# Placing W1's tables at the right end of SBUF and giving W3's and x's first loads earlier

## The chip, the cores and the metric

The kernel runs on one core of one Trainium2 chip. The metric is device time in microseconds (us) of one execution; lower is better. TensorE does matrix products, VectorE and ScalarE elementwise work, GpSimd a few small steps; SP (SyncE) and ScalarE give the DMA transfers.

## The reference

Three stages on 3072 tokens (4 sequences of 768), all weights in float64 for the host and taken apart on the chip:

```python
# 1. attention in chunks of 32 queries over 8 memory keys and 56 neighbours; 8 heads of 64
a = softmax(q_c @ k_full.T / 8);  x = a @ v_full          # x: 3072 x 512
# 2. first feed-forward: W1 512 x 1024, W2 1024 x 512
h = x @ W1;  solu = h * softmax(h)
x2 = (layernorm(solu) * g_ln) @ W2                        # x2: 3072 x 512
# 3. second feed-forward: W3 512 x 2048, W4 2048 x 512
h3 = x2 @ W3;  g = max(0.01 * h3, h3);  out = g @ W4
```

## The kernel before, in words

Every product is made of float32 parts: an operand is split into a high part (rounded, on ScalarE) and a low part (the rest, on VectorE), and three matmuls, high-high, high-low and low-high, go into one PSUM bank. A table is therefore always a pair such as `w1h`, `w1l`.

**Stages 1 and 2** run over 24 tiles of 128 tokens (`for i in range(NTILE + 1)`). For tile i the loop does attention of tile i+2, `s_h` (product with W1, softmax, LayerNorm: max, exp, product `so`, Square pass `e`/`ve`, `rstd`, scaling of `so`), `s_lt` (transposes, high and low part into `lhl`), a piece of W3's decoding (`load_raw`, `decode_steps`, `store_w3`: W3 is decoded, combined and stored to DRAM as `w3f`), and `s_o` for work i-5: one quarter (`ec`) of the product of a block of 512 tokens with W2 into bank `x2p`. `s_o` copies the bank to `x2s` on ScalarE (L355) and stores it to DRAM, `x2d` (L356). `x2s` has one buffer (`bufs=1`), so a copy waits for the store before it. Four such works (block 5) are left behind the loop: **W2's tail**, 96 matmuls.

**Stage 3** multiplies x2 with W3 and the result with W4 by Strassen-Winograd products P1 to P7. Tokens go in three pairs of blocks (v = 0, 1, 2). `load_xt` loads a pair from `x2d` in four transfers (b12, b22, b11, b21) into `xt` (pair 0) or `xtq` (pair 1), `x_steps` makes the seven operands by four additions or subtractions and seven splits (`split`, L503 on ScalarE, L504 on VectorE). `load_w3` loads a slot (`L0`, `L1`: W3's seven operands of 256 columns), `w3_steps` splits it (L561, L562). A unit is one slot with one pair: unit 0 is L0 with pair 0, unit 1 is L0 with pair 1. TensorE's order within a unit is P1, P5, P4 of the unit before, P6, P3 of the unit before, P2, P7. P1, P6, P7 and P4 add up in one bank C, and ScalarE keeps its state between them (`keep`, L677: s after P1, u after P6, g after P7). So P6 waits for s, P7 for u, P4 for g.

**Order.** Up to W2's tail a list scheduler places the instructions of TensorE, VectorE, ScalarE and GpSimd by the order of the program text and by when it takes operands to be ready; from `order_ctx` on SP's order is that of the text, and from the units on that of all engines. Each engine works through its own list in order. Each transfer adds to one of eight completion counters, given in turn in the order of the text; it waits until the transfer before it on that counter has landed.

**Memory.** A core's memory is a stack from the left and one from the right. Before, `w1h`, `w1l`, `w2h`, `w2l` lie at the left (16 KB per partition each), and L0 to L3 take their place after W2's tail: L0, L1 that of W1, L2, L3 that of W2. `xq` (with `xtq`) takes that of `lhl`. Pair 1's operands for P1, P5, P6, P2 are kept in L2 and L3 until those hold W4. `xr` (operands of pair 0) and `xt` take the place of stage 1's buffers at the right, among them those of W3's staging.

The lines that matter: L355 and L356, L497 (x loads), L503 to L522 (x steps), L553 (W3 load), L561 and L562, L648 (TensorE in stage 3), L677.

Of the kernel before, what the change touches and what calls it, by code (L numbers as in the profile page):

```python
# [9 lines left out]
F32 = mybir.dt.float32  # L10
F32R = mybir.dt.float32r
# [12 lines left out]
LAG = 5  # L24
# [15 lines left out]
def tile_kernel(  # L40
# [13 lines left out]
    P = 128  # L54
    NTILE = qt.shape[0]
# [5 lines left out]
    KD = DM // P  # L61
    KF = DFF // P
    KF2 = DFF2 // P
    BT = 512
    NBLK = NT // BT
    TB = BT // P
# [76 lines left out]


    sa, sh, satt, sps, sx2 = (ExitStack() for _ in range(5))
    wA = sa.enter_context(tc.tile_pool(name="wA", bufs=1, reuse_waits="tile"))
    w1h = wA.tile([P, 2, KD, 512], F32R, name="w1h")
    w1l = wA.tile([P, 2, KD, 512], F32R, name="w1l")
    w2h = wA.tile([P, KF, DM], F32R, name="w2h")
    w2l = wA.tile([P, KF, DM], F32R, name="w2l")  # L150
    sst = ExitStack()
# [45 lines left out]
    def s_scores(i, q, k):  # L197
        sc = ps_att.tile([P, 8, 64], F32, name="att")
        for hp in range(4):
            for c in range(4):  # L200
                cs = slice(32 * c, 32 * c + 32)
                nc.tensor.matmul(  # L202
                    sc[cs, 2 * hp : 2 * hp + 2, :], q[:, hp, cs], k[:, :, hp, c, :],
                    start=True, stop=True,
                )
        if i % TPB == 0:
            nc.vector.memset(sc[0:32, :, 8:24], NEG)
        if i % TPB == TPB - 1:
            nc.vector.memset(sc[96:128, :, 56:64], NEG)
        nms = sm.tile([P, 8], F32, name="nms")  # L210
        nc.vector.tensor_reduce(out=nms, in_=sc, op=ALU.max, axis=AX.X, negate=True)
        nc.vector.tensor_scalar_mul(nms, nms, SCALE)  # L212
        return sc, nms

    def s_exp(sc, nms):
        p = p1.tile([P, 8, 64], F32, name="p")
        rs = sm.tile([P, 8], F32, name="rs")
        for h in range(8):
            nc.scalar.activation(  # L219
                p[:, h], sc[:, h], AF.Exp, bias=nms[:, h : h + 1], scale=SCALE,  # L220
                accum_out=rs[:, h : h + 1],
            )
        return p, rs
# [118 lines left out]
    def s_o(b, ec, lh, ll, part):  # L342
        if part == 0:
            open_x2[ec] = ps_x2.tile([P, BT], F32, name="x2p")
        ps = open_x2[ec]
        es = slice(ec * P, (ec + 1) * P)
        for kk in range(4 * part, 4 * part + 4):
            for n, (a, r) in enumerate(((w2h, lh), (w2h, ll), (w2l, lh))):
                nc.tensor.matmul(  # L349
                    ps, a[:, kk, es], r[:, kk],  # L350
                    start=(kk == 0 and n == 0), stop=(kk == KF - 1 and n == 2),
                )
        if part == 1:
# [27 lines left out]
    for d in LOADS:  # L381
# [3 lines left out]
        n = int(d[1])  # L385
# [24 lines left out]
    lb = {}  # L410
# [20 lines left out]
    for i in range(NTILE + 1):  # L431
        a = i + 2
        b, t = divmod(i, TB)
# [4 lines left out]
        if att:  # L438
            p, rs = s_exp(*s_scores(a, ld[0], ld[1]))
# [13 lines left out]
        if so is not None:  # L453
            j = i - 1
# [10 lines left out]
        if 0 <= i - W3_FROM < KF2:  # L465
            f = i - W3_FROM
# [11 lines left out]
    store_w3(KF2 - 1, w3s)  # L478
    sps.close()
    satt.close()  # L480

    NPAIR, NV = KF2 // 2, NBLK // 2
    tt, pt_ = nc.vector.tensor_tensor, nc.gpsimd.tensor_tensor
    PROD = ("P1", "P5", "P6", "P2", "P7", "P3", "P4")
    SLOT = {"P1": 0, "P2": 1, "P7": 2, "P4": 3, "P5": 4, "P6": 5, "P3": 6}
    ACC = {"P1": "A", "P2": "A", "P5": "B", "P3": "B", "P6": "C", "P7": "C", "P4": "C"}
    ACC3 = {**ACC, "P1": "C"}
    spx, sxr, sxt, sl, sq, sd, sg, s4 = (ExitStack() for _ in range(8))
    ps = spx.enter_context(tc.tile_pool(name="ps_abc", bufs=2, space=PSUM, reuse_waits="tile"))
    xrp = sxr.enter_context(tc.tile_pool(name="xrp", bufs=1, side="right", reuse_waits="tile"))  # L490
    xr = {r: xrp.tile([P, 2, 2, BT], F32R, name=f"x{r}") for r in PROD}
    xtp = sxt.enter_context(tc.tile_pool(name="xtp", bufs=1, side="right", reuse_waits="tile"))

    def load_xt(v, tb):
        t = dict(zip(("b11", "b12", "b22", "b21", "t2"), (tb[:, n : n + 2] for n in range(0, 10, 2))))
        for n, b, k in (("b12", 1, 0), ("b22", 1, 2), ("b11", 0, 0), ("b21", 0, 2)):
            nc.sync.dma_start(out=t[n], in_=x2d[2 * v + b, :, k : k + 2])  # L497
        return t

    def x_steps(t, x):  # L500

        def split(r, src):
            nc.scalar.activation(x[r][:, 0], src, AF.Copy)  # L503
            tt(out=x[r][:, 1], in0=src, in1=x[r][:, 0].bitcast(F32), op=ALU.subtract)  # L504

        tt(out=t["b12"], in0=t["b22"], in1=t["b12"], op=ALU.subtract)
        yield
        tt(out=t["t2"], in0=t["b12"], in1=t["b11"], op=ALU.add)
        yield
        split("P1", t["b11"])  # L510
        yield
        tt(out=t["b11"], in0=t["b22"], in1=t["t2"], op=ALU.subtract)
        yield
        split("P5", t["b11"])
        yield
        split("P6", t["t2"])
        yield
        split("P2", t["b21"])
        yield
        split("P7", t["b12"])  # L520
        yield
        tt(out=t["b12"], in0=t["b21"], in1=t["t2"], op=ALU.subtract)  # L522
        yield
        split("P4", t["b12"])
        yield
        split("P3", t["b22"])
        yield
# [1 line left out]
    ENGS = {ENG.PE, ENG.DVE, ENG.Activation, ENG.Pool, ENG.SP}  # L529
    order_ctx = ExitStack()  # L530
    order_ctx.enter_context(tc.manual_schedule(engines={ENG.SP}))
    for i in range(NTILE + 1, NTILE + LAG):
        j = i - LAG
        s_o(j // TB, j % TB, *lb[j // TB], 0)
        s_o(j // TB, j % TB, *lb[j // TB], 1)
    sx2.close()
    sh.close()
    sa.close()
    regl = sl.enter_context(tc.tile_pool(name="regl", bufs=1, reuse_waits="tile"))
    reg = {n: regl.tile([P, 4096], F32R, name=n) for n in ("L0", "L1", "L2", "L3")}  # L540
    xq = sq.enter_context(tc.tile_pool(name="xq", bufs=1, reuse_waits="tile"))
    xtq = xq.tile([P, 10, BT], F32, name="xtq")
    W4_AT = {"P1": "N0", "P5": "N1", "P6": "L2", "P7": "L3", "P2": "L1", "P3": "L0", "P4": "R0"}
    xm = [xq.tile([P, 2048 * n], F32R, name=f"xm{n}") for n in (1, 2)]
    xl_ = {
        r: t[:, 2048 * h : 2048 * h + 2048].rearrange("p (a k t) -> p a k t", a=2, k=2)
        for r, t, h in zip(
            PROD, [reg["L2"]] * 2 + [reg["L3"]] * 2 + [xm[1]] * 2 + xm[:1], (0, 1, 0, 1, 0, 1, 0)
        )
    }  # L550

    def load_w3(q, n):
        nc.sync.dma_start(  # L553
            out=reg[n][:, 1792:3584].bitcast(F32), in_=w3f[q].rearrange("p r f -> p (r f)")
        )
        return reg[n]
# [11 lines left out]

    w3l = [load_w3(q, f"L{q}") for q in range(2)]
    xs0 = x_steps(load_xt(0, xtp.tile([P, 10, BT], F32, name="xt")), xr)  # L570
    xs1 = x_steps(load_xt(1, xtq), xl_)
    for _ in range(5):
        next(xs0)
# [60 lines left out]
    def load_w4(r):  # L634
        nc.sync.dma_start(
            out=reg[W4_AT[r]][:, 2048:4096].bitcast(F32), in_=w4f[SLOT[r]].rearrange("q p c -> q (p c)")
        )

    def w4_split(r):
        for n in range(2):  # L640
            h, l = (reg[W4_AT[r]][:, o + 1024 * n : o + 1024 * n + 1024] for o in (0, 2048))
            nc.scalar.activation(h, l.bitcast(F32), AF.Copy)
# [120 lines left out]
    for n, (q, v) in enumerate(units):  # L763
# [8 lines left out]
        k = n - NA  # L772
# [52 lines left out]
    hts += [hp.tile([P, 3, BT], F32R, name="h") for _ in range(2)]  # L825
    t2k += [hp.tile([P, BT], F32, name=f"t2k{n}", bufs=1) for n in range(1, NPAIR)]
    tp = s4.enter_context(tc.tile_pool(name="tp", bufs=1, side="right", reuse_waits="tile"))
    regr = s4.enter_context(tc.tile_pool(name="regr", bufs=1, side="right", reuse_waits="tile"))
    reg["R0"] = regr.tile([P, 4096], F32R, name="R0")

    split_g(1)

    def product(r, p, bh, bl, acc, es=range(2)):
        w = reg[W4_AT[r]].rearrange("q (h p c) -> q h p c", p=NPAIR, h=2)
        for e in es:
            ds = slice(e * P, e * P + P)
            three(
                acc[e], [w[:, 0, p, ds], w[:, 1, p, ds]], [bh, bl],
                r in ("P1", "P5", "P6") and p == 0, p == NPAIR - 1,
            )  # L840
# [8 lines left out]
    for n, (v, s, k) in enumerate(steps):  # L849
        h, l = halves.pop(n)  # L850
# [55 lines left out]
            store(NV - 1, 1, 0, e, s1[e], ts_, (nc.sync, nc.scalar)[n])  # L906
    order_ctx.close()
    s4.close()
    sl.close()
    spx.close()  # L910

# [46 lines left out]
```

## Time and profile before

| | us |
|---|---|
| median of 3 timed runs (lowest to highest) | 885.0 (884.75 to 885.45) |
| the profiled execution | 888.56 |
| its span | 886.7 |
| TensorE busy in it | 833.2 (94%) |
| VectorE busy | 643.9 (73%) |
| ScalarE busy | 471.9 (53%) |

The span runs from the first to the last instruction; the profiled execution's own time has what lies around it. A row that names a line in the form L503 speaks of the kernel above. In a timeline row the numbers are start and length in us; behind the operation stands output<-input, the shape, the count (x3), and in brackets how long the engine had been idle before and what ended that. PE is TensorE (PEld its weight loads), DVE VectorE, ACT ScalarE, POOL GpSimd, SP SyncE; SPq and ACTq are their issues of transfers.

### The profile page before, as it was taken

How to read it: one execution, taken by the hardware profiler on the slowest of the kernel's cores; microseconds unless marked ns; L12 is line 12 of the kernel's file. 1: busy time of each engine (PE TensorE's matmuls, PEld its weight loads, DVE VectorE, ACT ScalarE, POOL GpSimd, SP SyncE). 2: the span in 40 equal slices, each digit the busy share in tenths (PEclk: the TensorE clock that was granted, in tenths of full speed). 3: DMA queues.
4: the chain of work that ended last, by engine and by line, in shares of the span. 5: the costliest groups of instructions: out<-in, count | busy, mean ns of one | idle time of the engine just before them, and what ended most of it. 6: DMA issues, size and time to landing. Idle time of an engine off the chain costs nothing.

```text
span 886.7 us, 13628 instructions
## 1 busy us (share of the span) xinstructions
PE 833.2 (94%) x4960; PEld 660.8 (75%) x4960; DVE 643.9 (73%) x1145; ACT 471.9 (53%) x1067; POOL 56.5 (6%) x63
## 2 busy tenths in 40 slices
PE   3789999999999999965899999999999999999998
PEld 2467778677777778853688888878877888888886
DVE  4789987777887877619788854657488959658773
ACT  2477954445455454325556655577656635444542
POOL 2233310000000000000000000000000010010001
PEclk9999999999999999995899999999999999999999
DMA  9756786868788775462489866287768557546642
GB/s 228 182 162 194 197 229 207 269 204 247 210 255 246 217 214 178 160 187 82 149 312 333 344 232 231 96 297 275 301 253 319 179 178 224 191 151 233 202 150 95
DMA packets 69891, 190.95 MB, mean 215 GB/s; under 512 B 8000, under 2 KB 32064, under 8 KB 65856
## 3 DMA queue, kind: packets, MB, share of 16 engines
q1 hardware_dynamic: 56864, 175.14, 60.4%
q10 hardware_dynamic: 12960, 14.95, 5.8%
q8 instruction: 39, 0.64, 0.3%
q14 instruction: 28, 0.23, 0.1%
HBM read 129.24 MB, written 60.82 MB: 214 GB/s over the span
## 4 chain that ended last, share of the span: by engine, by line
PE 69%; DVE 13%; DMA 9%; ACT 5%; issue 2%; POOL 1%; SPq 0%; ACTq 0%; DVEq 0%; POOLq 0%
PE C L648 23%; PE B L648 13%; PE x2p L349 10%; PE A L648 9%; PE h L91 9%; DMA raw<-in_w 3%; DMA x2d<-x2s 2%; DMA lt<-lnd 2%; PE att L244 2%; PE att L202 1%; DMA ring<-gd 1%; ACT p L219 1%; DVE xP L504 1%; DVE so L288 1%; DVE hnm L280 1%
## 5 line engine op out<-in xcount | busy, mean ns | idle before, releaser
L349 PE MATMUL x2p<-lhl,w2h 128*128 128x512 f32 x384 | 127.2, 406 | 0.0
L648 PE MATMUL C<-xP,L 128*128 128x512 f32 x384 | 98.9, 399 | 16.9 <-ACT xP L503 9.1
L648 PEld LDWEIGHTS C<-xP,L 128*128 128x128 f32 x384 | 73.1, 192 | 35.2 <-ACT xP L503 9.5
L349 PEld LDWEIGHTS x2p<-lhl,w2h 128*128 128x128 f32 x384 | 70.3, 189 | 15.5 <-issue 2.0
L349 PE MATMUL x2p<-lhl,w2l 128*128 128x512 f32 x192 | 77.4, 403 | 0.0
L91 PE MATMUL h<-w1l,xh 128*128 128x512 f32 x168 | 67.7, 403 | 2.0 <-POOL w1l L134 1.9
L91 PE MATMUL h<-w1h,xh 128*128 128x512 f32 x168 | 69.0, 411 | 0.5 <-ACT w1h L133 0.5
L219 ACT ACTIVATE p<-att,nms 128x64 f32<-128x64 f32 x192 | 57.2, 321 | 22.4 <-DVE nms L212 22.1
L648 PE MATMUL C<-h,L 128*128 128x512 f32 x192 | 67.0, 390 | 0.1
L91 PE MATMUL h<-w1h,xl 128*128 128x512 f32 x168 | 66.9, 398 | 0.0
L759 DVE TENSOR_TENSOR ring<-ring,h 128x512 fp32r<-128x512 f32 x96 | 61.8, 685 | 3.5 <-ACT h L758 2.9
L674 ACT ACTIVATE g<-g 128x512 f32<-128x512 f32 x72 | 45.0, 626 | 26.0 <-DVE g L693 20.2
L293 ACT ACTIVATE e<-so,nmu 128x1024 f32<-128x1024 f32 x24 | 27.7, 1153 | 55.5 <-DVE nmu L291 55.1
L758 ACT ACTIVATE h<-ring 128x512 fp32r<-128x512 f32 x72 | 39.8, 622 | 32.1 <-DMA ring<-gd 17.5
L648 PE MATMUL B<-xP,L 128*128 128x512 f32 x192 | 51.6, 405 | 2.6 <-DVE xP L504 1.5
L562 DVE TENSOR_TENSOR L<-L 128x1024 fp32r<-128x1024 f32 (+1 forms) x28 | 30.2, 1083 | 25.2 <-ACT L L561 25.2
L693 DVE TENSOR_TENSOR g<-B,u 128x512 f32<-128x512 f32 x23 | 15.9, 690 | 42.6 <-PE B L648 42.6
L648 PEld LDWEIGHTS B<-xP,L 128*128 128x128 f32 x192 | 37.5, 196 | 12.1 <-DVE xP L504 2.0
L758 ACT ACTIVATE h<-t2k 128x512 fp32r<-128x512 f32 x48 | 28.6, 627 | 32.1 <-DVE t2k L751 18.1
L648 PEld LDWEIGHTS C<-h,L 128*128 128x128 f32 x192 | 36.0, 188 | 8.0 <-DVE u L873 0.5
L349 PEld LDWEIGHTS x2p<-lhl,w2l 128*128 128x128 f32 x192 | 36.2, 189 | 7.7 <-issue 1.0
L219 ACT ACTIVATION_READ_ACCUMULATOR p<-att,nms 128x1 f32 x192 | 41.1, 214 | 0.0
(183 smaller groups left out, 1912.1 us busy)
## 6 DMA issues: line engine op xcount, KB each, us to landing
ring<-gd SPq DMA_DIRECT2D x48, 768.0 KB, 4.1
gd<-g SPq DMA_DIRECT2D x24, 1024.0 KB, 5.0
raw<-in_w SPq DMA_DIRECT2D x32, 512.0 KB, 6.1
L<-w3f SPq DMA_DIRECT2D x14, 896.0 KB, 5.3
kbd<-in_kw SPq DMA_DIRECT2D x46, 256.0 KB, 4.7
vbd<-in_vw SPq DMA_DIRECT2D x46, 256.0 KB, 4.6
lnd<-sl SPq DMA_DIRECT2D x16, 512.0 KB, 4.0
lt<-lnd ACTq DMA_DIRECT2D x64, 128.0 KB, 3.3
```

The costliest lines, as they stand in the source:

```text
L91: nc.tensor.matmul(ps, a, b, start=(i == 0), stop=(i == 3 * n - 1))
L202: nc.tensor.matmul(sc[cs, 2 * hp : 2 * hp + 2, :], q[:, hp, cs], k[:, :, hp, c, :], start=True, stop=True,)
L219: nc.scalar.activation(p[:, h], sc[:, h], AF.Exp, bias=nms[:, h : h + 1], scale=SCALE, accum_out=rs[:, h : h + 1],)
L244: nc.tensor.matmul(xp[cs, 2 * hp : 2 * hp + 2, :], pt[:, hp, cs], v[:, :, hp, c, :], start=True, stop=True,)
L293: nc.scalar.activation(e, so, AF.Square, bias=nmu, accum_out=ve)
L349: nc.tensor.matmul(ps, a[:, kk, es], r[:, kk], start=(kk == 0 and n == 0), stop=(kk == KF - 1 and n == 2),)
L562: tt(out=l, in0=l.bitcast(F32), in1=h.bitcast(F32), op=ALU.subtract)
L648: nc.tensor.matmul(acc, w[i], x[j], start=first and n == 0, stop=last and n == 2, skip_group_check=True)
L674: nc.scalar.activation(u.g[:, i], u.g[:, i] if src is None else src, AF.Prelu, alpha=0.01)
L693: tt(out=o.g[:, 1], in0=o.acc["B"], in1=o.u2, op=ALU.add)
L758: nc.scalar.activation(h[:, i], src[n_], AF.Copy)
L759: tt(out=l[:, i], in0=src[n_], in1=h[:, i].bitcast(F32), op=ALU.subtract)
```

## The change

W1's two tables get a pool of their own at the right end of SBUF, opened before all the others there and closed behind stage 2. L0 and L1 get a pool at that place; L2 and L3 stay at the left, in W2's place. With that the loads of L0, L1 and of pair 0's `xt` no longer need memory of W2's tail, and the text gives them, with the generators of their steps, ahead of the four tail works.

```diff
+    sw1 = ExitStack()
+    wB = sw1.enter_context(tc.tile_pool(name="wB", bufs=1, side="right", reuse_waits="tile"))
+    w1h = wB.tile([P, 2, KD, 512], F32R, name="w1h")
+    w1l = wB.tile([P, 2, KD, 512], F32R, name="w1l")
     wA = sa.enter_context(tc.tile_pool(name="wA", bufs=1, reuse_waits="tile"))
-    w1h = wA.tile([P, 2, KD, 512], F32R, name="w1h")
-    w1l = wA.tile([P, 2, KD, 512], F32R, name="w1l")
...
     satt.close()
+    sw1.close()
...
+    regr = sr.enter_context(tc.tile_pool(name="regr", bufs=1, side="right", reuse_waits="tile"))
+    reg = {n: regr.tile([P, 4096], F32R, name=n) for n in ("L0", "L1")}
     xrp = sxr.enter_context(tc.tile_pool(name="xrp", bufs=1, side="right", reuse_waits="tile"))
...
     order_ctx.enter_context(tc.manual_schedule(engines={ENG.SP}))
+    def load_w3(q, n):
...
+    w3l = [load_w3(q, f"L{q}") for q in range(2)]
+    xs0 = x_steps(load_xt(0, xtp.tile([P, 10, BT], F32, name="xt")), xr)
     for i in range(NTILE + 1, NTILE + LAG):
         j = i - LAG
         s_o(j // TB, j % TB, *lb[j // TB], 0)
         s_o(j // TB, j % TB, *lb[j // TB], 1)
...
-    reg = {n: regl.tile([P, 4096], F32R, name=n) for n in ("L0", "L1", "L2", "L3")}
+    for n in ("L2", "L3"):
+        reg[n] = regl.tile([P, 4096], F32R, name=n)
...
-    w3l = [load_w3(q, f"L{q}") for q in range(2)]
-    xs0 = x_steps(load_xt(0, xtp.tile([P, 10, BT], F32, name="xt")), xr)
     xs1 = x_steps(load_xt(1, xtq), xl_)
```

The scheduler then orders the instructions around W2's tail anew. In the changed kernel L355 is L357, L497 is L502, L503 is L508, L553 is L538, L561 and L562 are L546 and L547, L648 is L654, and L677 is L683.

SP's list around the last W3 stores, before (L553 loads L0 and L1, L428 and L429 store W3, L497 loads x):

```order
L99 DMA raw<-in_w 128x4x256
L428 DMA w3f<-m 128x512
L429 DMA w3f<-w3s 128x768
L419 DMA w3f<-m 128x512
L428 DMA w3f<-m 128x512
L429 DMA w3f<-w3s 128x768
L553 DMA L_4305<-w3f 128x1792
L553 DMA L_4306<-w3f 128x1792
L497 DMA xt<-x2d 128x1024 x4
L497 DMA xtq<-x2d 128x1024 x4
```

The same place now:

```order
L99 DMA raw<-in_w 128x4x256
L430 DMA w3f<-m 128x512
L431 DMA w3f<-w3s 128x768
L538 DMA L_4179<-w3f 128x1792
L538 DMA L_4180<-w3f 128x1792
L421 DMA w3f<-m 128x512
L430 DMA w3f<-m 128x512
L431 DMA w3f<-w3s 128x768
L502 DMA xt<-x2d 128x1024 x4
L502 DMA xtq<-x2d 128x1024 x4
```

The loads of L0 and L1 moved ahead of three stores; the x loads kept their place among SP's transfers, but not their counters: before, the second to fourth xt load and the first xtq load followed stores of W2's tail on their counters; now of these eight only the third xtq load does.

ScalarE's list from the last LayerNorm's Square pass (`e,ve`) on, before (four of the five x2s copies belong to the tail):

```order
L109 ACTIVATE m<-raw 128x512
L355 ACTIVATE x2s<-x2p 128x512
L356 DMA x2d<-x2s 128x512
L293 ACTIVATE e,ve<-so,nmu 128x1024
L313 ACTIVATE lhl<-tr 128x4x128 x2
...
L355 ACTIVATE x2s<-x2p 128x512
L356 DMA x2d<-x2s 128x512
L561 ACTIVATE L_4305<-L_4305 128x1024
L561 ACTIVATE L_4305<-L_4305 128x768
L503 ACTIVATE xP_4180<-xt 128x1024
L503 ACTIVATE xP_4179<-xt 128x1024
```

The same stretch now, its beginning and the middle of the tail:

```order
L109 ACTIVATE m<-raw 128x512
L546 ACTIVATE L_4179<-L_4179 128x1024
L546 ACTIVATE L_4179<-L_4179 128x768
L357 ACTIVATE x2s<-x2p 128x512
L358 DMA x2d<-x2s 128x512
L295 ACTIVATE e,ve<-so,nmu 128x1024
...
L508 ACTIVATE xP_4189<-xt 128x1024
L508 ACTIVATE xP_4188<-xt 128x1024
L357 ACTIVATE x2s<-x2p 128x512
L508 ACTIVATE xP_4184<-xt 128x1024
L358 DMA x2d<-x2s 128x512
```

L0's split (L561, now L546) moved from behind the tail's last copy to a place ahead of the last LayerNorm's Square pass, and pair 0's splits stand between the tail's copies; xP_4184, the operand of P1, stands between a copy and its store.

VectorE's list at the last LayerNorm, now (L547 is L0's low half, L296 and L303 the end of the LayerNorm, L427 to L429 W3's combination, L316 lhl's low half):

```order
L111 TENSOR_SCALAR m<-m 128x512
L547 TENSOR_TENSOR L_4179<-L_4179 128x1024
L115 TENSOR_SCALAR m<-m 128x512
L547 TENSOR_TENSOR L_4179<-L_4179 128x768
L296 TENSOR_SCALAR ve<-ve 128x1
L119 SCALAR_TENSOR_TENSOR m<-raw,m 128x512
L303 TENSOR_SCALAR so<-so,nmu,rstd 128x1024
L124 SCALAR_TENSOR_TENSOR m<-raw,m 128x512
L426 TENSOR_TENSOR w3s<-m 128x256
```

Before, L547's two rows stood behind all this, as L562, and the two passes L119 and L124 ahead of `ve`.

## Rows read from the trace of the kernel before

**Rows 1.** The page's 40 slices: TensorE's granted clock in tenths of full speed
```profile
PEclk9999999999999999995899999999999999999999
```

**Rows 2.** Busy time by stretch; columns as the first line says
```profile
core 0: us, PE busy (x) PEld busy (x) DVE busy (x) ACT busy (x) POOL busy (x), PEclk, DMA share, GB/s
357.10:361.60 4.50, 4.50 (x25) 3.85 (x24) 4.47 (x9) 3.33 (x7) 0.00 (x0) 1.00 0.00 0
392.30:401.30 9.00, 0.00 (x0) 0.00 (x0) 5.23 (x5) 5.30 (x7) 0.00 (x0) 0.78 0.55 173
430.18:432.90 2.72, 2.72 (x6) 2.15 (x7) 2.58 (x6) 1.52 (x3) 0.00 (x0) 0.50 0.00 0
435.21:445.00 9.79, 9.79 (x45) 8.07 (x43) 7.76 (x16) 5.05 (x9) 0.00 (x0) 1.00 0.62 215
```

**Rows 3.** Waits, 366 to 425: total us, times, longest
```profile
ACT x2s L355 <- DMA x2d<-x2s: 21.1, 4, 8.0
```

**Rows 4.** SP's timeline, 368 to 402
```profile
371.97 17.27 SPq L497 DMA_DIRECT2D xt<-x2d  x4
393.96 7.30 SPq L497 DMA_DIRECT2D xtq<-x2d  x4
```

**Rows 5.** ScalarE's timeline, 330 to 402
```profile
363.41 0.60 ACT L355 ACTIVATE x2s<-x2p 128x512 f32<-128x512 f32 x1 [2.33 <-PE x2p L349]
...
393.98 0.60 ACT L355 ACTIVATE x2s<-x2p 128x512 f32<-128x512 f32 x1 [4.39 <-DMA x2d<-x2s]
...
394.98 1.79 ACT L561 ACTIVATE L<-L 128x1024 fp32r<-128x1024 f32 x2 [0.40 <-ACT x2s L355]
```

**Rows 6.** Timeline of all engines, 396 to 445
```profile
396.07 2.09 DVE L562 TENSOR_TENSOR L<-L 128x1024 fp32r<-128x1024 f32 x2 [25.23 <-ACT L L561]
...
401.39 0.80 PE L648 MATMUL C<-xP,L 128*128 128x512 f32 x1 [9.12 <-ACT xP L503]
...
409.44 1.22 DVE L506 TENSOR_TENSOR xtq<-xtq 128x1024 f32<-128x1024 f32 x1
...
414.09 1.23 DVE L512 TENSOR_TENSOR xtq<-xtq 128x1024 f32<-128x1024 f32 x1
...
419.16 0.57 ACT L677 ACTIVATE u<-C 128x512 f32<-128x512 f32 x1
...
419.78 1.65 PE L648 MATMUL C<-xP,L 128*128 128x512 f32 x6 [1.17 <-ACT u L677]
...
426.58 1.68 PE L648 MATMUL C<-xP,L 128*128 128x512 f32 x6 [2.42 <-ACT g L677]
...
430.18 2.93 PE L648 MATMUL C<-L,L 128*128 128x512 f32 x6 [1.91 <-ACT s L677]
```

**Rows 7.** TensorE's timeline, 335 to 372: W1's last matmul, the last transposes
```profile
356.65 0.39 PE L91 MATMUL h<-w1h,xl 128*128 128x512 f32 x1
...
368.26 1.06 PE L311 MATMUL tr<-ident,so 128*128 128x128 f32 x8 [0.58 <-DVE so L301]
```

**Rows 8.** The chain of waits: a run of 24 matmuls of W2
```profile
346.15 5.44 PE x2p L349 x24
```

**Rows 9.** VectorE's timeline, 330 to 372, in the last LayerNorm
```profile
364.07 0.42 DVE L111 TENSOR_SCALAR m<-m 128x512 f32<-128x512 f32 x1
...
366.32 0.15 DVE L294 TENSOR_SCALAR ve<-ve 128x1 f32<-128x1 f32 x1
```

**Rows 10.** Transfers given near 363.9, 369.7, 371.2, 394.6: KB each, us to landing
```profile
x2d<-x2s ACTq DMA_DIRECT2D x1, 256.0 KB, 2.4
...
L<-w3f SPq DMA_DIRECT2D x1, 896.0 KB, 5.7
...
x2d<-x2s ACTq DMA_DIRECT2D x1, 256.0 KB, 7.8
...
x2d<-x2s ACTq DMA_DIRECT2D x1, 256.0 KB, 5.8
```

**Rows 11.** Line 553, the 14 loads of W3 slots
```profile
DMA to landing us min/median/max: 4.4/5.3/8.1
```

More of the change, by code (lines that the diff above doesn't have):

```diff
@@ L487, in tile_kernel @@
     ACC3 = {**ACC, "P1": "C"}
-    spx, sxr, sxt, sl, sq, sd, sg, s4 = (ExitStack() for _ in range(8))
+    spx, sxr, sxt, sl, sr, sq, sd, sg, s4 = (ExitStack() for _ in range(9))
     ps = spx.enter_context(tc.tile_pool(name="ps_abc", bufs=2, space=PSUM, reuse_waits="tile"))
+    regr = sr.enter_context(tc.tile_pool(name="regr", bufs=1, side="right", reuse_waits="tile"))
+    reg = {n: regr.tile([P, 4096], F32R, name=n) for n in ("L0", "L1")}
     xrp = sxr.enter_context(tc.tile_pool(name="xrp", bufs=1, side="right", reuse_waits="tile"))
@@ L531, in tile_kernel @@
     order_ctx.enter_context(tc.manual_schedule(engines={ENG.SP}))
[L532 to L539, printed above, removed]
-    reg = {n: regl.tile([P, 4096], F32R, name=n) for n in ("L0", "L1", "L2", "L3")}
[L541 to L550, printed above, removed]
     def load_w3(q, n):
@@ L570, in tile_kernel @@
     xs0 = x_steps(load_xt(0, xtp.tile([P, 10, BT], F32, name="xt")), xr)
+    for i in range(NTILE + 1, NTILE + LAG):
+        j = i - LAG
+        s_o(j // TB, j % TB, *lb[j // TB], 0)
+        s_o(j // TB, j % TB, *lb[j // TB], 1)
+    sx2.close()
+    sh.close()
+    sa.close()
+    regl = sl.enter_context(tc.tile_pool(name="regl", bufs=1, reuse_waits="tile"))
+    for n in ("L2", "L3"):
+        reg[n] = regl.tile([P, 4096], F32R, name=n)
+    xq = sq.enter_context(tc.tile_pool(name="xq", bufs=1, reuse_waits="tile"))
+    xtq = xq.tile([P, 10, BT], F32, name="xtq")
+    W4_AT = {"P1": "N0", "P5": "N1", "P6": "L2", "P7": "L3", "P2": "L1", "P3": "L0", "P4": "R0"}
+    xm = [xq.tile([P, 2048 * n], F32R, name=f"xm{n}") for n in (1, 2)]
+    xl_ = {
+        r: t[:, 2048 * h : 2048 * h + 2048].rearrange("p (a k t) -> p a k t", a=2, k=2)
+        for r, t, h in zip(
+            PROD, [reg["L2"]] * 2 + [reg["L3"]] * 2 + [xm[1]] * 2 + xm[:1], (0, 1, 0, 1, 0, 1, 0)
+        )
+    }
     xs1 = x_steps(load_xt(1, xtq), xl_)
@@ L827, in tile_kernel @@
     tp = s4.enter_context(tc.tile_pool(name="tp", bufs=1, side="right", reuse_waits="tile"))
-    regr = s4.enter_context(tc.tile_pool(name="regr", bufs=1, side="right", reuse_waits="tile"))
-    reg["R0"] = regr.tile([P, 4096], F32R, name="R0")
+    regr0 = s4.enter_context(tc.tile_pool(name="regr0", bufs=1, side="right", reuse_waits="tile"))
+    reg["R0"] = regr0.tile([P, 4096], F32R, name="R0")
     split_g(1)
@@ L908, in tile_kernel @@
     s4.close()
+    sr.close()
     sl.close()
```

## The prediction

> **What bounds the kernel now.** I read the page's slices of TensorE's granted clock first: 9 throughout, but for two neighbouring slices of 5 and 8 [rows 1]. Two slices of 40 are some 44 us, so one place, near 400 to 440 us, differs from the rest. The busy times by stretches show it: between 392.3 and 401.3 TensorE does nothing; at 430.18 its clock is at 0.50, the lower level of 1.2 GHz; from 435.21 on it is at 1.00, without idle time [rows 2]. The place begins with the end of W2's tail and ends before 435.
>
> Who is late there? The waits show 21.1 us of ScalarE's copies x2s behind their own stores x2d [rows 3]. SP's timeline gives the other half: the four xt loads of pair 0 are spread over 17.27 us from 371.97, the four xtq loads of pair 1 begin at 393.96 [rows 4]. The store of 371.16 landed after 7.8 us [rows 10], at 379.0, and the second xt load went out then: a transfer waits for the one before it on its completion counter, and in the order of before those are the stores of W2's tail. ScalarE ends this chain: its last x2s copy starts at 393.98, the split of L0 only at 394.98 [rows 5]. From there VectorE carries everything: L0's low half at 396.07, pair 0's steps, pair 1's first step at 409.44, its subtraction b11 at 414.09; then come u, the copy that releases bank C, at 419.16, and TensorE's P7 at 419.78, P4 at 426.58 and P6 of the second unit at 430.18 [rows 6].
>
> **The change, part by part.** L0 and L1 now lie where W1's tables were, free after the last matmul of W1 at 356.65 + 0.39 = 357.0 [rows 7], and their loads are given ahead of the last three w3f stores. Behind their wait on SP stands a w3f store; nothing was moved between 357.1 and 361.6 [rows 2], so nothing is late by it. With L1 beside it L0 took 5.7 us [rows 10] behind other stores; on an empty queue I take 5: it lands at 362.
>
> *Cost ahead of the tail.* L0's split, 1.79 us on ScalarE [rows 5] and 2.09 on VectorE [rows 6], now stands inside the last LayerNorm. On ScalarE it falls into an idle time of 2.33 us that ended at 363.41 [rows 5]. On VectorE it stands between L111 at 364.07 and ve at 366.32 [rows 9]: two subtractions and one pass over m from 364.5 end at 364.5 + 2.09 + 0.43 = 367.0, so ve is 0.65 late. Three small W3 steps ahead of lhl's low half, and the first matmul of the second tail tile (it waits for an x2s copy, and the rest of the tail is queued behind it on TensorE), add some 0.35. The tail ended at 401.39 - 9.12 = 392.3 [rows 6]; it will end at 393.3. Bounds: 0, when TensorE's own wait of 0.58 [rows 7] and its other work cover it; +3, when L0 takes the longest time of a W3 load, 8.1 us [rows 11], and lands at 365.
>
> *Loads and stores.* xt lies in W3's staging, so its first load still waits for W3's store: 372.6 against 371.97, no gain. The other three no longer wait for tail stores and follow within some 1.5 us; pair 1's loads follow as those land, since their memory is free.
>
> The chain of stores stays, x2s having one buffer. A store takes 2.4 us alone, 5.8 beside two loads, 7.8 behind L0 and L1 [rows 10]. Store 1 goes out at 371.5 beside the xt loads; I take 5.8: 377.3, copy until 378. Store 2, beside the rest of xt and two xtq loads, 5.8: 384. Copy, then xP1's split of about 1 us, which now stands between copy and store 3: 385.7, and 5.8 again: 391.5. Copy, store 4 alone, 2.4: 394.6. So the last copy starts at X = 394.6, hardly other than 393.98, but pair 0's work is no longer behind it: the splits run on ScalarE between the copies, their low halves on a VectorE that sat idle for 25.23 us there [rows 6]. Bounds of X: 393.3, the tail's end, when all stores are short; 402, when stores 1 to 3 take 7.8 and the fourth 4.4, the wait in [rows 5]. I take 394.6, nearest to the row with two loads beside a store.
>
> *After the tail.* TensorE does P1 and P5 of unit 0 without a wait, 1.4 us each (24 matmuls take 5.44 [rows 8]). The copy s of bank C starts 0.65 after the last x2s copy, and not before xP4's low half, whose memory it takes: splits xP5 and xP4 on ScalarE from 392.1 to 394.2, subtraction until 395.4. So S = 395.4. Then pair 1: s 0.6, b11's split 1.05, its low half 1.2, and the subtraction b11 starts at S + 2.85 = 398.25, where before had 414.09 [rows 6]. From there the order on ScalarE and VectorE is that of before, and VectorE is the late one in it, so u, P7, P4 and P6 keep their distances: all 414.09 - 398.25 = 15.8 us earlier. Behind 435 TensorE's order is the same and it is full: the gain is carried to the end.
>
> *The clock.* TensorE will idle for some 5 us between P2, near 399, and P7, near 404. The mean clock over 9.0 idle us was 0.78 [rows 2], so it fell inside that gap; it may be low at P7. Three products stand there, 4.1 us at the upper level, 8.2 at the lower, and P4 may start only 6.8 us after P7 (426.58 - 419.78 [rows 6]): 1.4 us can be lost. On the other side P6 took 2.93 at the lower level [rows 6] where 1.4 is full speed; if the clock is up there, 1.5 come back, and some 0.8 in the product behind. I take 0, between -2.3 and +1.4.
>
> **Sum.** The profiled execution took 888.56 us, its span 886.7: 888.56 - 15.8 = 872.8. It was 3.56 slower than the median of the three timed runs, 885.0 (the lowest 884.75); against that median it is 885.0 - 15.8 = 869.2 us.
>
> **Rivals.** In all of them the gain is 414.09 - (S + 2.85), that is 411.24 - S.
> A. The store chain crawls: with more loads beside them stores 1 to 3 take 7.8 us each. X = 402, S = 402.7, gain 8.5: 876.5. For it: the one store with two large loads ahead took that. Against: those were 896 KB each and already under way.
> B. The clock is up at P6: 15.8 + 2.3, 866.9. For it: TensorE idles some 2 us there, where before it had 2.42 and 1.91 around P4. Against: it must first rise at P7.
> F. The loads don't hold the stores up: each takes 2.4 or little more, X is the tail's end, s waits for P1 alone at 394.7, gain 16.5: 868.5. Against: the 7.8 us of 371.16.
> By a rule of the Trainium skill (DMA: Bandwidth & Descriptors, "Queues, rings and completion order") F is what should happen: each DMA engine takes the rings of the two issuing engines in turn, so ScalarE's store need not wait out SP's loads. The store of 371.16 does not look like that, those of 5.8 us could.
> C. The change doesn't do what it says, the x loads still hanging on the tail's stores: only L0's 2 us leave VectorE's chain and 1 us is paid in the LayerNorm: 884. Against: in the new order their counters belong to earlier transfers.
> D. Slower: ScalarE stands at L0's split, and the copy and Square of the last LayerNorm stand behind it. Each us that L0 lands after 363 moves the tail's end by one. The gain is gone when the tail ends at 409.8 (S = 411.24), that is with L0 at about 379, 22 us after its issue; at 382 the time is 888. For it: nothing else in the order is as exposed. Against: the queue is empty then, and no W3 load took over 8.1 us [rows 11].
> E. Partial losses: the LayerNorm 3 us late, the clock low through P4, two stores slow: 872.5 to 882.
>
> **How the numbers follow.** Forecast 53% (own range 867.5 to 872); A 15%; B 10%; F 9%; E 8%; C 2%; D 3%. The range reaches from below B, 865.5, to near A, 875.5; half of A and E, and C and D lie beyond, with a little below: under 20%. A measurement of this kernel can tell about 0.2%, 1.8 us, from no change: faster 0.95 (forecast, A, B, E, F), same 0.02 (part of C), slower 0.03 (D).
>
> **What would show it.** Right: TensorE goes from the tail into P1 without a gap; the xt loads go out within 2 us of each other near 373; L0's split near 362; the tail's end near 393; pair 1's first step on VectorE near 396 instead of 409.44; P7 near 404, and the distances from there on kept. Wrong: the last x2s copy after 398 (A) or at the tail's end (F), P6 short (B), xt loads spread over 17 us (C), ScalarE idle before L0's split after 363 (D), or any stretch behind 440 that differs, since I let all of it just move.

## The result and the profile after

| | us |
|---|---|
| changed kernel, median of 4 runs (lowest to highest) | 870.77 (869.75 to 871.68) |
| kernel before, 4 runs on the same chip | 885.23 (884.75 to 885.67) |
| ratio, 95% interval | 0.9837 (0.9819 to 0.9854) |
| profiled execution of the changed kernel, its span | 871.68, 869.9 |
| forecast | 869.2 (865.5 to 875.5) |

The change gained 14.46 us; 15.8 were forecast. In the profile after, W1's last matmul starts at 355.20, before at 356.65 [rows 7]. The work up to there is the same, so I compare distances from that row. The line numbers have moved: L357 is the copy x2s, L358 its store, L502 the x loads, L508 and L509 the splits, L511 to L527 the x steps, L538 the W3 load, L546 and L547 its split, L654 stage 3's matmuls, L683 `keep`.

The page's slices of the granted clock, to be held against [rows 1]: of the two low ones, 5 and 8, one of 8 is left.

```profile
PEclk9999999999999999998999999999999999999999
```

Busy time by stretch, columns as the first line says (before: [rows 2]):

```profile
core 0: us, PE busy (x) PEld busy (x) DVE busy (x) ACT busy (x) POOL busy (x), PEclk, DMA share, GB/s
355.59:360.15 4.56, 4.56 (x25) 3.91 (x24) 4.49 (x9) 2.73 (x6) 0.00 (x0) 1.00 0.73 269
...
397.60:403.20 5.60, 0.10 (x1) 0.00 (x1) 4.48 (x4) 4.38 (x5) 0.00 (x0) 0.74 0.19 60
403.20:406.00 2.80, 2.80 (x7) 2.22 (x8) 2.52 (x3) 0.22 (x1) 0.00 (x0) 0.50 0.19 73
...
418.00:430.00 12.00, 12.00 (x54) 9.94 (x53) 9.90 (x19) 5.70 (x10) 0.00 (x0) 1.00 0.67 229
```

Where the DMA engines had moved nothing for 4.5 us they now carry L0 and L1. The idle 9.0 us behind the tail have become 5.5 us between P2 and P7 of unit 0 (5.60 of that stretch, less 0.10 busy). Behind them the clock is at 0.50, the lower of its two levels, and from 418 on TensorE is full.

SP's timeline (before: [rows 4]):

```profile
355.65 0.80 SPq L538 DMA_DIRECT2D L<-w3f  x2
...
371.24 2.79 SPq L502 DMA_DIRECT2D xt<-x2d  x4
376.64 6.97 SPq L502 DMA_DIRECT2D xtq<-x2d  x4
```

The four xt loads go out in 2.79 us instead of 17.27, the xtq loads begin 16 us earlier by their distance. ScalarE's timeline (before: [rows 5]):

```profile
360.15 1.80 ACT L546 ACTIVATE L<-L 128x1024 fp32r<-128x1024 f32 x2 [0.53 <-DMA L<-w3f]
...
375.52 0.60 ACT L357 ACTIVATE x2s<-x2p 128x512 f32<-128x512 f32 x1 [5.84 <-PE x2p L351]
...
382.88 0.60 ACT L357 ACTIVATE x2s<-x2p 128x512 f32<-128x512 f32 x1 [2.43 <-DMA x2d<-x2s]
...
389.49 0.60 ACT L357 ACTIVATE x2s<-x2p 128x512 f32<-128x512 f32 x1 [3.17 <-DMA x2d<-x2s]
...
392.55 0.60 ACT L357 ACTIVATE x2s<-x2p 128x512 f32<-128x512 f32 x1
...
394.04 0.60 ACT L683 ACTIVATE s<-C 128x512 f32<-128x512 f32 x1 [0.89 <-DVE xP L509]
...
411.87 0.63 ACT L680 ACTIVATE g<-g 128x512 f32<-128x512 f32 x1 [1.92 <-DVE g L703]
```

L0 landed at 360.1, 4.5 us after its issue. Two copies wait for a store, 5.6 us where four had waited 21.1 [rows 3]. The last copy stands directly behind two splits of ScalarE; behind it s waits 0.89 us for VectorE's low half.

The transfers by their issue (KB, us to landing; before: [rows 10]): the stores of 369.70, 376.14, 383.51 and 390.12, behind which the tail's four copies stand.

```profile
x2d<-x2s ACTq DMA_DIRECT2D x1, 256.0 KB, 4.0
...
x2d<-x2s ACTq DMA_DIRECT2D x1, 256.0 KB, 6.7
...
x2d<-x2s ACTq DMA_DIRECT2D x1, 256.0 KB, 5.9
...
x2d<-x2s ACTq DMA_DIRECT2D x1, 256.0 KB, 2.3
```

VectorE's and TensorE's timelines behind the tail (before: [rows 6]):

```profile
378.13 1.23 DVE L511 TENSOR_TENSOR xt<-xt 128x1024 f32<-128x1024 f32 x1 [7.46 <-DMA xt<-x2d]
...
391.59 2.36 DVE L509 TENSOR_TENSOR xP<-xt,xP 128x1024 fp32r<-128x1024 f32 x2 [1.36 <-ACT xP L508]
393.86 1.22 DVE L511 TENSOR_TENSOR xtq<-xtq 128x1024 f32<-128x1024 f32 x1
395.12 1.22 DVE L513 TENSOR_TENSOR xtq<-xtq 128x1024 f32<-128x1024 f32 x1
396.26 1.22 DVE L509 TENSOR_TENSOR L<-xtq,L 128x1024 fp32r<-128x1024 f32 x1
397.51 1.23 DVE L517 TENSOR_TENSOR xtq<-xtq 128x1024 f32<-128x1024 f32 x1
...
409.15 2.08 DVE L547 TENSOR_TENSOR L<-L 128x1024 fp32r<-128x1024 f32 x2
```

```profile
391.41 1.52 PE L654 MATMUL C<-xP,L 128*128 128x512 f32 x6
...
403.20 2.93 PE L654 MATMUL C<-xP,L 128*128 128x512 f32 x6 [5.50 <-ACT u L683]
...
410.00 1.64 PE L654 MATMUL C<-xP,L 128*128 128x512 f32 x6 [0.56 <-ACT g L683]
413.58 2.60 PE L654 MATMUL C<-L,L 128*128 128x512 f32 x6 [1.94 <-ACT s L683]
...
419.39 1.52 PE L654 MATMUL C<-xm,L 128*128 128x512 f32 x6
```

VectorE works on pair 0 from 378.13 instead of sitting idle until 396.07. P1 follows the tail without a wait. P7 of unit 0 stands 48.00 us behind W1's last matmul instead of 63.13, P6 of unit 1 58.38 instead of 73.53. The product of the last row, P7 of unit 1, is the first that is full in both kernels; before it stood here:

```profile
436.60 1.53 PE L648 MATMUL C<-xm,L 128*128 128x512 f32 x6
```

That is 64.19 us behind W1's last matmul against 79.95: 15.76 gained in the stage. Behind it everything only moves: from there to the end of the span pass 450.5 us, before 450.1.

### The profile page after: what moved, and what is told of

Same layout as the page of the kernel before. It is cut to its first block, busy times and chain, and to the rows that moved or that the text cites. A ratio compares the mean times of both kernels' runs of the same rounds, so it can differ in the third digit from the quotient of the medians.

```text
span 869.9 us, 13633 instructions
## 1 busy us (share of the span) xinstructions
PE 827.6 (95%) x4960; PEld 658.1 (76%) x4960; DVE 643.4 (74%) x1145; ACT 472.2 (54%) x1067; POOL 56.6 (7%) x63
## 4 chain that ended last, share of the span: by engine, by line
PE 74%; DVE 12%; DMA 6%; ACT 4%; issue 2%; POOL 1%; SPq 0%; ACTq 0%; DVEq 0%; POOLq 0%
PE C L654 24%; PE B L654 14%; PE x2p L351 12%; PE A L654 10%; PE h L91 9%; DMA raw<-in_w 2%; PE att L246 2%; PE att L204 2%; DMA x2d<-x2s 1%; DMA ring<-gd 1%; DVE so L290 1%; ACT p L221 1%; DMA kbd<-in_kw 1%; DVE m L124 1%; PE tr L260 1%
## 5 line engine op out<-in xcount | busy, mean ns | idle before, releaser
L654 PE MATMUL C<-xP,L 128*128 128x512 f32 x384 | 97.4, 395 | 7.5 <-ACT u L683 5.9
L654 PEld LDWEIGHTS C<-xP,L 128*128 128x128 f32 x384 | 72.4, 190 | 24.9 <-ACT u L683 6.7
L654 PE MATMUL C<-h,L 128*128 128x512 f32 x192 | 67.0, 390 | 0.0
L654 PE MATMUL B<-xP,L 128*128 128x512 f32 x192 | 49.7, 395 | 0.2 <-DVE g L709 0.2
L654 PEld LDWEIGHTS B<-xP,L 128*128 128x128 f32 x192 | 36.5, 191 | 8.6 <-DVE g L709 0.6
L654 PEld LDWEIGHTS C<-h,L 128*128 128x128 f32 x192 | 36.0, 188 | 7.9 <-DVE u L879 0.4
L91 PEld LDWEIGHTS h<-w1h,xh 128*128 128x128 f32 x168 | 31.8, 189 | 11.6 <-issue 3.2
```

Of the source, the lines that this page charges most:

```text
L91: nc.tensor.matmul(ps, a, b, start=(i == 0), stop=(i == 3 * n - 1))
L654: nc.tensor.matmul(acc, w[i], x[j], start=first and n == 0, stop=last and n == 2, skip_group_check=True)
```

## The experiments

"Distance" is us from the start of W1's last matmul in the same profile. The timed median stands with its ratio to the kernel before, timed beside it on the same chip, whose median was 885.2 to 887.0.

| kernel | s | P7 of unit 1 | median | ratio (95% interval) |
|---|---|---|---|---|
| before | 56.37 | 79.95 | 885.23 | 1 |
| changed | 38.84 | 64.19 | 870.77 | 0.9837 (0.9819 to 0.9854) |
| changed, once more | 40.04 | 65.40 | 870.63 | 0.9833 (0.9807 to 0.9859) |
| x loads moved alone | 46.65 | 71.37 | 880.18 | 0.9921 (0.9892 to 0.9951) |
| W1 moved alone | 38.78 | 62.53 | 871.75 | 0.9829 (0.9795 to 0.9863) |
| L0, L1 behind the x loads | 41.21 | 65.96 | 872.07 | 0.9822 (0.9775 to 0.9869) |
| second place for a copy | 38.35 | 61.47 | 867.55 | 0.9769 (0.9739 to 0.9798) |
| L1's split later | 39.22 | 60.43 | 869.74 | 0.9796 (0.9768 to 0.9824) |
| both | 37.76 | 58.37 | 863.44 | 0.9756 (0.9729 to 0.9784) |
| changed, with filler | 39.46 | 63.22 | 869.44 | 0.9823 (0.9786 to 0.9861) |
| both, with filler | 37.75 | 58.35 | 865.39 | 0.9782 (0.9749 to 0.9815) |

**The x loads moved alone.** In the kernel before:

```diff
+    xs0 = x_steps(load_xt(0, xtp.tile([P, 10, BT], F32, name="xt")), xr)
     for i in range(NTILE + 1, NTILE + LAG):
...
-    xs0 = x_steps(load_xt(0, xtp.tile([P, 10, BT], F32, name="xt")), xr)
```

Expected:

> The kernel before with one line moved: the x loads of pair 0 and their splits stand ahead of W2's tail. W1's tables stay at the left, the loads of L0 and L1 stay behind the tail. Theory 1 (what cost the time before is that the xt loads went out behind the tail's stores, and so pair 0's splits behind the tail): the xt loads go out within 3 us of each other near 372, pair 0's splits stand between the x2s copies, TensorE goes from the tail into P1 without a gap; nothing is lost in the last LayerNorm (the tail ends 1 us earlier than in the changed kernel), but L0's split, 1.8 us on ScalarE and 2.1 on VectorE, stands behind the last x2s copy and makes the copy s of bank C up to 2 us later. So 871 to 874 us, about the changed kernel. Theory 2 (the freed memory of W1, by which L0 and L1 are loaded and split ahead of the tail, carries the gain): at most 3 us of it is here, 882 or more.

Measured: 6.8 us of gain, between the theories. SP's timeline:

```profile
371.20 2.59 SPq L497 DMA_DIRECT2D xt<-x2d  x4
378.44 0.80 SPq L554 DMA_DIRECT2D L<-w3f  x2
379.33 14.52 SPq L497 DMA_DIRECT2D xtq<-x2d  x4
```

ScalarE's and TensorE's:

```profile
378.46 0.60 ACT L355 ACTIVATE x2s<-x2p 128x512 f32<-128x512 f32 x1 [6.75 <-DMA x2d<-x2s]
...
398.41 0.60 ACT L355 ACTIVATE x2s<-x2p 128x512 f32<-128x512 f32 x1 [2.75 <-DMA x2d<-x2s]
...
399.41 1.79 ACT L562 ACTIVATE L<-L 128x1024 fp32r<-128x1024 f32 x2 [0.40 <-ACT x2s L355]
```

```profile
400.52 3.33 PE L648 MATMUL C<-xP,L 128*128 128x512 f32 x6 [7.05 <-ACT L L562]
403.65 2.76 PE L648 MATMUL B<-xP,L 128*128 128x512 f32 x6
```

Theory 1 is right on the x loads: they go out in 2.59 us, and pair 0 is split beside the tail. What it missed is L0. Its load goes out at 378.44, in the same moment as the copy that waits for the store of 371.74 to land: the load's counter belonged to that store, though its memory had been free for 20 us. (The profile's waits put 4.6 us of SP's wait for this load down to that store; the load neither reads nor writes what the store touches, and in the built program that store is the transfer before it on its counter.) So 1.75 MB are loaded beside the tail. The next store takes 7.9 us, and the last copy comes at a distance of 41.17, not 37.35: 3.8 us. Then L0's split stands ahead of P1, TensorE idles 7.05 us, and P1 and P5 take 3.33 and 2.76 us at the lower clock; with that s is 7.8 us later than in the changed kernel: 3.8 up to the last copy, 4.0 behind it.

**W1 moved alone.** The changed kernel with the same line put back behind the tail.

Expected:

> The changed kernel with the x loads of pair 0 put back in the text behind the tail; W1's tables stay at the right end and L0 and L1 are loaded ahead of the tail. Theory 1 (only the place among SP's instructions and the transfers that a load's counter belonged to before matter; with L0 and L1 out of the way SP's order of loads and their counters come out the same): 870.8 within 1.5 us, xt loads near 371 within 3 us of each other. Theory 2 (the place in the text sets when the x loads go out): they go out behind the tail's stores, spread over 15 us or more, and the time is 882 to 885 us.

```profile
372.08 2.73 SPq L502 DMA_DIRECT2D xt<-x2d  x4
...
414.36 1.65 PE L654 MATMUL C<-L,L 128*128 128x512 f32 x6 [1.92 <-ACT s L683]
```

Theory 1 holds: 2.73 us, and a time that can't be told from the changed kernel's. (The second row, P6 of unit 1, is for the part on the clock.) In the built program the lists of all engines and the counters are those of the changed kernel, so this is one more measurement of it. That corrects a sentence of the section on the order: the counters follow the order in which the scheduler places the transfers, not that of the text. The kernel before gave the loads of L0 and L1 at 369.69 already; what changes for the x loads is the place of these two among all transfers. With them placed ahead of the tail, the x loads behind them on SP are placed early by themselves. Of the two parts of the change, W1's move, with the loads of L0 and L1 ahead of the tail, carries all; the line of the x loads alone, without it, is worth 7 us.

**L0 and L1 behind the x loads.** The changed kernel with two lines swapped:

```diff
-    w3l = [load_w3(q, f"L{q}") for q in range(2)]
     xs0 = x_steps(load_xt(0, xtp.tile([P, 10, BT], F32, name="xt")), xr)
+    w3l = [load_w3(q, f"L{q}") for q in range(2)]
```

Expected:

> The changed kernel with the loads of L0 and L1 given right behind the x loads of pair 0 instead of at the end of W1; memory and the rest as in the changed kernel. They go out near 374, and L0's split, 1.8 us on ScalarE and 2.1 on VectorE, stands between the tail's x2s copies, not ahead of P1. Theory 1 (two loads of 896 KB beside the tail's stores make these slow, which is 3.7 of the 7.7 us by which the kernel with the x loads moved alone had its copy s of bank C later): the stores of 369.7 and 376.1 take 7.5 to 8.5 us instead of 6.7 and 5.95, the last x2s copy and s come 2 to 4 us later, and the time is 872.5 to 875 us. Theory 2 (the stores are slow from the x loads anyway, and only L0's split between the last copy and P1, with the clock low behind that gap, cost that kernel its time): s within 1 us of the changed kernel's, 870 to 872 us; the last LayerNorm gets its 0.8 us back.

Transfers given at 378.01 and 386.05, and the whole DMA traffic from 369 to 393; the same traffic in the changed kernel behind it:

```profile
x2d<-x2s ACTq DMA_DIRECT2D x1, 256.0 KB, 7.3
...
x2d<-x2s ACTq DMA_DIRECT2D x1, 256.0 KB, 6.7
...
DMA packets 2020, 7.21 MB, mean 300 GB/s; under 512 B 230, under 2 KB 230, under 8 KB 2018
```

```profile
DMA packets 2018, 5.92 MB, mean 247 GB/s; under 512 B 224, under 2 KB 224, under 8 KB 2016
```

The stores took 7.1, 7.3, 6.7 and 2.3 us instead of 4.0, 6.7, 5.9 and 2.3, and s is 2.4 us later than in one profile of the changed kernel, 1.2 later than in the other. That is the direction of theory 1, with less per store. All four copies of the tail wait for a store here, where two did in the changed kernel. The time, 872.07 (867.5 to 873.78), doesn't tell the theories apart. So in this order the load beside the stores costs the chain 1 to 2.5 us. In the kernel with the x loads alone, where L0 went out later, it was up to 3.8 of the 7.8; the other 4.0 lie behind the last copy, where L0's split stands ahead of P1 and the clock is low behind the gap. (P7 of unit 0 in the kernel with the swap, for the last section:)

```profile
405.44 1.64 PE L654 MATMUL C<-xP,L 128*128 128x512 f32 x6 [2.38 <-ACT u L683]
```

**A second place for one copy, and L1's split later.** Two edits of the changed kernel, against waits that its profile still shows:

```diff
-        s_o(j // TB, j % TB, *lb[j // TB], 1)
+        s_o(j // TB, j % TB, *lb[j // TB], 1, reg["L1"][:, 3584:] if j == NTILE - 3 else None)
...
-            s = lp.tile([P, BT], F32, name="x2s", bufs=1)
+            s = lp.tile([P, BT], F32, name="x2s", bufs=1) if spare_s is None else spare_s
...
-            nc.scalar.dma_start(out=x2d[b, :, ec, :], in_=s)
+            nc.scalar.dma_start(out=x2d[b, :, ec, :], in_=s if spare_s is None else s.bitcast(F32))
```

```diff
-    urgent, delayed = [xs1, w3_steps(w3l[1])], []
+    urgent, delayed = [xs1], [(7, w3_steps(w3l[1]))]
```

Expected of the first:

> The changed kernel with a second place for one of the tail's x2s copies: that of the last but two is put into columns of L1's region that are unused then and stored from there. That quarter of one block of x2 is rounded to the high part's format. ScalarE's waits of 2.43 and 3.17 us for stores in the tail go away or shrink to under 1 us. Theory 1 (the store chain ends at the last copy and binds xP1's split, xP4's low half, s and b11 in turn): s starts near 392.5 to 393 instead of 394.04 and the subtraction b11 1.5 to 2.3 us earlier than 397.51, so 868.5 to 869.3 us. Theory 2 (VectorE's own work of the low halves, or the tail's end on TensorE at 391.5, binds by then): under 0.7 us of gain, 870 to 871.5 us.

ScalarE with the second place:

```profile
386.54 0.60 ACT L357 ACTIVATE x2s<-x2p 128x512 f32<-128x512 f32 x1 [0.83 <-PE x2p L351]
...
392.89 0.60 ACT L357 ACTIVATE x2s<-x2p 128x512 f32<-128x512 f32 x1 [1.43 <-DMA x2d<-x2s]
...
393.95 0.60 ACT L683 ACTIVATE s<-C 128x512 f32<-128x512 f32 x1 [0.46 <-DVE xtq L511]
```

The two waits are gone, one of 1.43 us has come at the last copy. s is 0.4 us earlier and P7 of unit 1 1.1 us, both against the run with W1 alone, which had the same clock there. The other 0.6 lie between s and b11. There pass 3.47 us in all five profiles with the changed kernel's order up to there (the three of the changed kernel, L1's split later, filler), since VectorE is late. Here VectorE waits for ScalarE again:

```profile
395.52 1.23 DVE L509 TENSOR_TENSOR L<-xtq,L 128x1024 fp32r<-128x1024 f32 x1 [0.41 <-ACT L L508]
```

and 2.84 pass, as in the two kernels with both edits. One pair of profiles says little of s: over all of them it comes at 37.75 to 38.35 with the second place (three) and at 38.78 to 40.04 without (five), and b11 at 40.59 to 41.19 against 42.25 to 43.51. That is 2.0 us earlier on the mean, the size of theory 1, and theory 2 is too small. The median is 4.2 us below that of the run with W1 alone, more than either theory gave. The two profiled executions are 1.4 us apart, this one the slowest of its five and that one the fastest of its four, and of the 1.4 the trace accounts for 1.1; the remainder lies in runs without a profile.

Expected of the second:

> The changed kernel with L1's split taken later: it stands behind a later product of unit 0 in the order of ScalarE and VectorE and no longer ahead of the copy g that P4 waits for. Theory 1 (1.05 to 1.9 us of ScalarE and 1.2 to 2.1 of VectorE stand in the chain b11, u, g, P4, P6 of unit 1): g starts 1.0 to 1.9 us earlier, P4 and P6 of unit 1 too, and the time is 869 to 869.8 us. Theory 2 (P4's other operands, or a later product that needs L1, take the wait over): the same sum of idle time on TensorE behind the tail, 870.3 to 871.5 us. Theory 3: the late split stands ahead of something that is due, and the time is 872 or more.

```profile
409.68 1.52 PE L654 MATMUL C<-xP,L 128*128 128x512 f32 x6
411.39 1.65 PE L654 MATMUL C<-L,L 128*128 128x512 f32 x6 [0.19 <-ACT s L683]
```

P7 of unit 1 comes 2.1 us earlier than with W1 alone, and the time is 2.0 us lower, as theory 1 said. Counted from b11, which stands ahead of L1's split in both kernels, the copy g comes 1.1 us earlier, in theory 1's range. P4 gains only 0.7 of it, since it now follows P5 directly, and P6 of unit 1 gains 2.5: its wait of 1.94 us for s is 0.19. The theory didn't have this wait. In the changed kernel VectorE had done L1's low half, 2.08 us from 409.15, ahead of the step on bank A (`g`) behind which ScalarE's s stood: the wait of 1.92 us at 411.87.

Expected of both:

> The changed kernel with both edits: the second place for the x2s copy of the last but two (that quarter of one block of x2 is rounded to the high part's format), and L1's split taken behind a later product. If the two stand in different parts of the chain, their gains add up: from the tail's end to the third product of unit 1, 23.93 and 22.87 us with one edit each and 24.96 with none, so some 21.9 with both, and 2.5 to 3.7 us below the changed kernel. If one hides the other: 1.5 to 2.2 us below it.

P7 of unit 1 at 58.37, 4.2 us earlier than with W1 alone, 5.8 and 7.0 earlier than in the two profiles of the changed kernel; the median is 7.2 below the changed kernel's beside it, where 2.5 to 3.7 were expected. The gains add up, and to more than the sum that was expected: of the 4.2 us, 1.0 are at s, 0.6 between s and b11, 2.5 behind b11; s came 0.6 us earlier than with the second place alone, and that is within what s varies. Against the changed kernel, 0.9756 to 0.9833, the intervals don't overlap; against the second place alone they do. The price, as with the second place alone, is one quarter of one block of x2 rounded to the high part's format.

**The clock.** The changed kernel, and that with both edits, with 20 matmuls more between P2 and P7 of unit 0:

```diff
+            if u.n == 0 and j == 6:
+                for n in range(FILL):
+                    nc.tensor.matmul(idle, reg["L0"][:, 0:P], xr["P1"][:, 0, 0], start=n == 0, stop=n == FILL - 1)
             w3_product(w, r)
```

Expected of the first:

> The changed kernel with 20 matmuls more, whose result nobody reads, on TensorE between P2 and P7 of unit 0: about 4.5 us of work inside the 5.5 us for which it idles there. Theory 1 (the clock falls because TensorE idles, and the two products behind the gap are slow for that): P7 and the first product of unit 1 take 1.4 to 1.5 us each instead of 2.93 and 2.13. Since P4 waits for the copy g, not for TensorE, it starts no earlier, so nothing is gained up to there; P6 of unit 1 takes 1.65 instead of 2.60, as in the run that had the same instructions and the clock up there. Time: 0 to 1.7 us below the changed kernel. Theory 2 (the clock goes by something else): P7 still takes 2.9 us and the time is the same. Theory 3 (the filler delays P7): 1 us or more above the changed kernel.

```profile
394.69 4.69 PE L692 MATMUL idle<-xP,L 128*128 128x512 f32 x20
400.34 1.67 PE L655 MATMUL C<-xP,L 128*128 128x512 f32 x6 [0.95 <-ACT u L684]
...
407.14 2.93 PE L655 MATMUL C<-xP,L 128*128 128x512 f32 x6 [2.38 <-ACT g L684]
```

The clock stays up over the gap: P7 takes 1.67 instead of 2.93. But g comes when it came, 15.34 us behind s in both, so TensorE only waits for it 2.38 us instead of 0.56, and then it is P4 that takes 2.93. P6 of unit 1 takes 1.65, as theory 1 said. The median is 1.2 us below the changed kernel's, and the runs (865.03 to 876.34) don't tell them apart.

Expected of the second:

> The kernel with both edits, and the 20 matmuls more between P2 and P7 of unit 0. With L1's split out of the way the products P7, P1 and P5 of unit 1 end 0.5 us behind the copy g that P4 waits for, so here the low clock is on the path: with it up, P4 starts some 0.4 to 0.6 us earlier and the time is 0.3 to 0.8 us below the kernel with both edits, which is near what five rounds can tell. If the clock is not the bound: the same.

```profile
403.50 1.66 PE L655 MATMUL C<-xP,L 128*128 128x512 f32 x6 [1.28 <-ACT g L684]
405.66 1.67 PE L655 MATMUL C<-L,L 128*128 128x512 f32 x6 [0.50 <-ACT s L684]
```

The granted clock is 1.00 over the whole execution, P4 starts 0.9 us earlier than without the filler, and P6 gives it back at once by its wait for s. P7 of unit 1 stands at 58.35 against 58.37. So the 0.3 to 0.8 us that were expected with the clock as the bound did not come; the medians, 865.39 against 863.44, lie closer together than the runs of either kernel. The low clock at P7 costs nothing in either kernel, since the chain on ScalarE and VectorE is as late.

**The changed kernel once more.** Expected:

> The changed kernel once more, to stand beside the others on the same chip: 0.982 to 0.985 of the kernel before. P6 of unit 1 takes either 2.6 us (low clock) or 1.65 us; which of the two is open, since the same instructions gave both.

0.9833 (0.9807 to 0.9859). P6 of unit 1 took 2.15 us and P3 behind it 2.65: the low clock again, a little later.

## Why the prediction was right, point by point

- **Ahead of the tail.** Forecast +1.0 us, bounds 0 and 3. L0 took 4.5 us against 5, its split fell where it was put. The tail ends at a distance of 36.37 (391.57) against 35.63 before [rows 6, 7]: +0.7.
- **Loads and stores.** xt loads within 2.79 us against 1.5. Stores of 5.8, 5.8, 5.8 and 2.4 were taken; they were 4.0, 6.7, 5.9 and 2.3. The last copy was put at a distance of 37.95 and came at 37.35, as late as before, with pair 0 no longer behind it: [rows 3, 10] carried this term. That it met so well is in part luck. The forecast let every copy wait for a store; only two did. The tail's first copy waited for its matmuls until 375.52, 1.8 us behind the landing of its store, and the last stood behind splits that ended at 392.51, as its store landed. The 1 us for the split between a copy and its store was not paid: that store is given 0.63 us behind its copy, like the others.
- **s.** Forecast distance 38.75, bound by xP4's low half. Measured 38.84, bound by just that. In the second profile 40.04: there the store given next to the first xtq load took 8.1 us instead of 6.7, and the copy behind it came 1.4 us later by its distance.
- **b11.** Forecast 41.6, measured 42.31. This term was mis-sized: I counted 2.85 us from s on, by ScalarE. VectorE had 2.36 us of low halves until 393.86 and then three steps of pair 1 before b11, without a pause until 397.51; the VectorE queue set it, not s. From s to b11 passed 3.47 us; where VectorE was not late (the second place, L0 and L1 behind the x loads, the x loads alone) 2.83 to 2.84 did, as counted.
- **From b11 to TensorE.** Distances kept: 15.13 us of gain at b11 (57.44 against 42.31), 15.13 at P7, 15.15 at P6.
- **The clock.** Taken as 0, low at P7 and at P6. It was low at both. That at P7 costs nothing, as the fillers show. From P6 to P7 of unit 1 passed 5.81 us; in the run with W1 alone, whose instructions are the same, the clock was up and 4.21 passed, so the low clock costs 1.6 there. Before, 6.42 passed: 0.6 came back.
- **Sum.** 15.8 forecast, 15.76 in the stage of this profile, 14.55 and 17.42 in the two others with the same lists; 14.46 and 15.3 between the medians, measured twice. The forecast of 869.2 was 1.6 us too low. Mechanism and place are shown; 1.6 us is within what the stage itself varies, and there is only one profile of the kernel before. That 15.76 meets 15.8 is luck in its decimals: b11 gained 0.7 less than forecast, and 0.6 came back from the clock, which the sum had at 0.

The rivals: A fell (last copy at a distance of 37.35, A had 45.4). C fell: the x loads came off the stores. D fell: ScalarE waited 0.53 us for L0. B came true in one profile of three. E is there in parts only: 0.7 in the LayerNorm, the clock low at P6, one store of 8.1. F fell: two stores beside x loads took 6.7 and 5.9 us in one profile and 8.1 and 5.7 in the other, alone 2.3. The time could not have told it, since F's 868.5 lies 0.7 us from the forecast. By the Trainium skill (DMA: Bandwidth & Descriptors, "Queues, rings and completion order") each DMA engine goes round the queues that have work, a packet from each in turn; the trace agrees with that as sharing, two and a half to three and a half times the time alone, and not with F's reading that a store beside loads stays short.

One thing the prediction did not ask was which half of the edit does it. It treated the early W3 loads as preparation and the x loads as the gain. The runs show that the first brings the second by itself, and that the second without the first gives 6.8 us, less than half.

## What to carry to other kernels

When a load is late, look at what stands before it in its queue and on its completion counter, and not only at its own memory: with the two loads ahead of them placed earlier, the x loads came early too. Where an engine's chain binds, a wait taken off another engine (here TensorE's, by the filler) is given back at the next product. Measure stages from a row that the change doesn't touch.

## What was not expected of the hardware

- The same instruction lists gave P6 of unit 1 at 2.60, 1.65 and 2.15 us. After idle times of the same length, 2.38 us, a product took 2.93 us in the kernel with filler and 1.64 (P7 of unit 0) in the one with L0 and L1 behind the x loads. Ahead of the gap the first had run at the upper level; the second stood behind two products of 2.93 and 2.76 us, at the lower. The length of the gap alone doesn't tell what the clock does; what decides it stays open.
- The store given next to the first xtq load took 6.7 us in one profile of the changed kernel and 8.1 in the other.
- W1's last matmul started between 351.07 and 357.24 in the eleven profiles, at 355.20, 352.92 and 356.04 in the three of the changed kernel's lists. One profile can be 3 us off before the changed place is reached.
